# A block kernel with a full-length key buffer, other engines for some steps, and another table of issue

## The chip, the cores and the metric

The kernel runs on one core of one Trainium2 chip. The metric is the device time of one execution in microseconds (us). Three executions of the kernel before took 210.84, 212.09 and 212.49 us; the median is 212.09 us.

The engines are TensorE (PE, and PEld for its weight loads), VectorE (DVE), ScalarE (ACT), GpSimd (POOL) and SyncE (SP), which issues nearly all DMAs. Each runs its own instructions in order and waits on semaphores for the others.

## The reference, cut to what matters

```python
# x: 2048 tokens x 512; H = 32 heads of 16; W, dil = 8, 2; F = 1792
mod = silu(c) @ w_mod                          # six rows: sa, ca, ga, sb, cb, gb
h = layernorm(x) * (1 + ca) + sa
q, k, v = split(h @ wqkv)
# token s attends to the 8 tokens s, s-2, ..., s-14 of its own head
logits = einsum(q, k[s - 2*w]) * 16**-0.5      # masked before token 0
o = einsum(softmax(logits), v[s - 2*w])
x = x + ga * (o @ wo)
h = layernorm(x) * (1 + cb) + sb
h = layernorm(h)
u = gelu(einsum('bsd,sf->bdf', h, w1) + b1)    # mixes the tokens, not the channels
y = einsum('bdf,fs->bds', u, w2) + b2
x = x + gb * transpose(y)
```

Everything is bf16 in memory; sums are kept in f32.

## The kernel before, in words

The 2048 tokens are 16 tiles of 128, in five chunks of 2, 4, 4, 4 and 2 tiles (numbered 0 to 4; SIZES, L255). For each chunk `build_chunk` (L587 to L865) adds the steps below. The name of a step is what the table of issue uses, and a suffix says the engine.

- First norm: `ln1s` (statistics of a tile, DVE or ACT), `rstd1`, `nb1` (minus mean times scale, DVE), `n1_<tile>` (the norm itself; `ln_norm`, L397, on ACT, DVE or POOL). Then transposes, on PE for chunks 0 and 1, by DMA (`xt`) for the others.
- Projections: `qkv<chunk>_<t><j>` with t = 0, 1, 2 for query, key, value; each is four matmuls of 128x128 weights per group of channels. `ev` takes the result from PSUM to the query tile, the key tile `k_f` or the value tile.
- Attention: `qk` (DVE, products of query and shifted keys, a 128x4096 product tile in the four `big` buffers), `red` (PE, sums over the channels of a head), `max` (DVE), `sub` (PE), `exp` (ACT), `esum` (sum of the eight weights, PE, or DVE for chunk 4), `rcp` (ACT), `smB` (DVE), `a2` (four DMAs that spread the weights), `vd` (DMAs that spread the values), `pv` (DVE products), `pvacc` (PE sums), `oev` (copy out of PSUM).
- Output: `wo<tile>` (PE, four matmuls, and a fifth with the identity that adds the residual where `x1` runs on ACT), `x1_<tile>` (back to `xx`).
- Second and third norm: `ln2q`, `ln2m`, `rstd2`, `nb2`, `n2_<tile>`, `aff` (DVE, two passes: times 1 + cb, plus sb), `ln3s`, `rstd3`, `nb3`, `h3_<tile>`.

The token MLP runs over 14 feature tiles: `mlp1_<sweep>_<feature>_<first token tile>` as its tokens become ready, in three sweeps over the tokens, with `park` and `padd` holding partial sums in `gT`; then `gelu`, `mlp2_<token tile>`, `fin` (DVE) and `st_out` (DMA).

Keys of a chunk need the last 16 columns of the chunk before. `k_f` (L308, L309) is a buffer of ten tiles that chunks 3 and 4 write from its start again, so chunk 3 needs a copy of the last 16 key columns of chunk 2, `halo_k3` (L706, ACT). `qk3` reads that copy. For the values there are two buffers and four copies, `halo_v1` to `halo_v4`.

What sets the order of the work is `ORDER` (L180 to L237): one list of all 783 steps, written out in full. `_Graph.schedule` (L87) goes through it, gives out PSUM buffers (six) and product buffers, and the instructions are emitted in exactly this order, so each engine's queue is the list cut down to its engine. A suffix picks the engine: `:a` ACT, `:d` DVE, `:p` POOL, `:s` left out. `:q` has the step's matmuls made as four matmuls of 32 output partitions each (`mm`, L501) in place of one of 128. `warm0` to `warm5` (L507) are matmuls on the identity that compute nothing.

```python
def mm(out, lhsT, rhs, **kw):
    if not G.quad:
        return nc.tensor.matmul(out, lhsT=lhsT, rhs=rhs, **kw)
    for j in range(0, P, 32):
        nc.tensor.matmul(out[j:j + 32], lhsT=lhsT[:, j:j + 32], rhs=rhs, tile_position=(0, j), **kw)
```

Of the kernel before, what the change touches and what calls it, by code (L numbers as in the profile page):

```python
# [185 lines left out]
wsc1_0:p ln1s11:d ln1s6:a ln1v6 ln1s10:d qkv0_00 ev0_00:a qkv0_02 qkv1_03 ln1v9 qkv0_10 rstd1_2 ld_wmod2 ev0_02:a
ln1v11 ev0_10:a nb1_2 n1_7:p ev1_03:a warm3:s qkv1_01 n1_6:a qkv0_12 ld_wmod5 ev0_12:a ln1s13:d ln1s15:a ld_b1
ev1_01:a ln1s14:d qkv1_13 qkv1_11 ev1_11:a qk0_1 qvb1 qk0_0 qkv0_20 red0_0 red0_1 qk0_2 ln1v15 ld_wo0 qkv0_22:q xt6
ev1_13:a ld_wo2 qvb_cp1 ev0_20:a n1_9:p red0_2 ln1v14 ld_wo3 qkv1_23:q qk0_3 red0_3 n1_8:a mask qk1_1 max0 qkv1_00
qkv1_10 ln1v10 xt7 warm5:s ln1s12:a ln1v12 rstd1_4 ln1v13 ev0_22:a vd0_1 ev1_00:a xt8 sub0 exp0 ev1_10:a qk1_3 qk1_0  # L190
qkv1_02 ev1_02:a esum0 rcp0 xt9 smB0 ev1_23:a modrow nb1_4 mrows:a ld_row0 qkv1_12 ev1_12:a qk1_2 wsc1_3:a wsc1_2:a
rstd1_3 nb1_3 n1_10:a wsc2_0:a woq_s qkv1_22 wsc1_1:p red1_0 qkv2_02:q red1_1 red1_2 red1_3 max1 wsc2_2:a qkv1_21:q
a2_0_1 ev1_21:a qkv1_20:q halo_v1:p a2_0_2 sub1 qkv2_12 ev1_20:a exp1 ev2_12:a ev2_02:a qkv2_11 esum1 a2_0_0 a2_0_3
pv0_1 vd0_3 pv0_3 vd0_0 vd0_2 pv0_0 qkv2_03 xt10 n1_12:a xt12 rcp1 pvacc0_0 ev2_11:a pv0_2 qkv2_01 smB1 ev1_22:a
ev2_01:a ld_w1_0_0 pvacc0_1 pvacc0_2 oev0_0:a pvacc0_3 oev0_2:a a2_1_3 wsc2_3:a qk2_2 qkv2_00 ev2_00:a qkv2_10
# [5 lines left out]
vd2_3 oev1_1:a qkv3_20 qkv3_12 ev3_13:a qkv3_02 ln3s1:a oev1_2:a ln3s0:a xt14 wo5 ev3_12:a halo_v3:a qk3_0 xt15
ev3_02:a x1_5:a vd2_0 wo2 x1_2:a ln3v1 wo4 x1_4:a red3_0 ln2q5 smB2 qk3_1 ln2q4 wo3 x1_3:a ln2q3 ln3v0 rstd3_0 qk3_2
vd2_1 ln2q2 a2_2_0 a2_2_3 qkv4_00 qkv3_21 qkv4_12 qk3_3 ev4_12:a qkv4_22 a2_2_1 red3_1 nb3_0 ev4_00:a a2_2_2 h3_0:a
ev3_20:a ev3_21:a vd2_2 ev4_22:a pv2_0 ln2m2 rstd2_2 pv2_1 qkv3_23 qkv4_02 nb2_2 ev4_02:a h3_1:p ev3_23:a qkv3_22
ev3_22:a vd3_2 ln2m4 red3_2 red3_3 max3 pv2_2 pv2_3 n2_3:a n2_2:p pvacc2_0 oev2_0:a sub3 aff2 qk4_3 qkv4_20 exp3
rstd2_4 pvacc2_1 oev2_1:a qkv4_10 ev4_20:a ev4_10:a pvacc2_2 oev2_2:a nb2_4 esum3 rcp3 pvacc2_3 biascols ld_row3
biascols_cp:a n2_5:p vd3_0 vd3_3 oev2_3:a ln3s2:a n2_4:a ln3s3:d ln3v3 wo8 ln3v2 rstd3_2 smB3 a2_3_3 wo9 x1_9:a a2_3_0
nb3_2 h3_2:a wo6 h3_3:a qk4_0 wo7 x1_7:a mlp1_0_1_0 mlp1_0_2_0 halo_v4:a aff4 ln3s5:a qk4_2 ln3s4:d mlp1_0_6_0 vd3_1
red4_0 mlp1_0_5_0:q x1_8:a mlp1_0_3_0:q x1_6:a ln3v5 ln3v4 rstd3_4 ln2q9 qk4_1 red4_1 nb3_4 h3_4:a h3_5:a red4_2
red4_3 mlp1_0_0_0 mlp1_0_0_4 a2_3_2 a2_3_1 vd4_0 mlp1_0_3_4 pv3_1 ln2q8 ld_w2_4 ld_w2_1 ln2q7 mlp1_0_1_4 park0_0:a  # L210
park0_1:a mlp1_0_2_4 ln2q6 park0_2:a max4 mlp1_0_6_4 pvacc3_1 mlp1_0_8_0:q oev3_1:a pv3_3 mlp1_0_5_4:q ld_w1_0_1152
sub4:q ld_w2_3 ln2m6 rstd2_6 exp4 pv3_0 nb2_6 pv3_2 mlp1_0_4_0:q mlp1_0_4_4:q park0_3:a n2_7:p park0_4:a pvacc3_3
oev3_3:a vd4_1 mlp1_0_7_0:q ld_w2_2 pvacc3_0 park0_5:a oev3_0:d n2_6:a mlp1_0_9_0:q n2_8:a pvacc3_2 ld_w1_0_1408
oev3_2:a esum4 park0_6:a wo10 wo11 n2_9:p aff6 rcp4 smB4 a2_4_3 x1_10:a ln2q10 ln3s8:d wo12 ln3s7:d ln3v7 x1_11:a
ln3s6:a ln3s9:d wo13 vd4_3 ln3v8 ln3v6 ln3v9 x1_12:a ln2q12 ln2m10 rstd3_6 ln2q11 a2_4_0 mlp1_0_11_0 nb3_6 h3_8:a
a2_4_1 h3_7:p h3_6:d rstd2_10 x1_13:a mlp1_0_12_0:q warm4:s mlp1_0_10_0:q h3_9:a a2_4_2 mlp1_0_7_4:q vd4_2 ln2m11
rstd2_11 ln2q13 mlp1_0_9_4:q mlp1_0_8_4:q mlp1_0_8_8:q mlp1_0_7_8:q ld_w1_0_1664 park0_7:a park0_8:a ln2m12
mlp1_0_10_4:q pv4_1 mlp1_0_10_8:q pv4_2 nb2_11 mlp1_0_9_8:q mlp1_0_12_4:q mlp1_0_12_8:q n2_11:p ln2m13 pvacc4_2 pv4_3
pvacc4_3 pv4_0 nb2_10 pvacc4_0 pvacc4_1 park0_9:a mlp1_0_11_4:q ld_w1_1_0 rstd2_13 n2_10:d nb2_13 aff10 n2_13:p
rstd2_12 nb2_12 ld_w2_0 mlp1_0_11_8 oev4_2:a ln3s10:d ln3v10 oev4_0:a wo15 park0_10:a aff11 rstd3_10 nb3_10 wo14  # L220
# [10 lines left out]
gelu12 padd1_13 gelu13 mlp2_2_0 mlp2_0_0 mlp2_0_0b ld_w2_7 mlp2_8_0 ld_w2_9 ld_w2_11 mlp2_11_0 ld_w2_15 mlp2_0_0c
fin2_0 mlp2_5_0 fin0_0 mlp2_4_0 st_out0_0 fin4_0 st_out4_0 st_out2_0 mlp2_9_0 fin8_0 mlp2_1_0 fin1_0 st_out1_0
mlp2_3_0 fin3_0 mlp2_7_0 st_out3_0 mlp2_6_0 fin5_0 ld_w2_13 st_out5_0 fin6_0 st_out8_0 st_out6_0 fin9_0 fin7_0
st_out9_0 mlp2_12_0 mlp2_13_0 mlp2_10_0 mlp2_14_0 st_out7_0 fin12_0 st_out12_0 fin11_0 fin13_0 st_out13_0 mlp2_15_0
fin10_0 st_out10_0 fin14_0 st_out11_0 fin15_0 st_out15_0 mlp2_15_2 st_out14_0 fin15_2 st_out15_2 mlp2_15_1 fin15_1
# [775 lines left out]
```

## Time and profile before

| | |
|---|---|
| three executions | 210.84, 212.09, 212.49 us |
| span of the profiled execution, first to last instruction | 207.6 us |
| PE busy | 190.1 us (92%), 1630 matmuls |
| DVE busy | 160.5 us (77%) |
| ACT busy | 128.4 us (62%) |
| POOL busy | 30.6 us (15%) |
| mean granted TensorE clock | 0.999 |
| moved by DMA | 35.93 MB, mean 173 GB/s |

The span leaves out what lies before the first and after the last instruction; the median of the executions is 4.5 us above it. Every instruction is recorded by one helper, so all carry the line L131 and are told apart by their tiles. In lists by time the first two columns are the start and the length in us; "[2.72 <-ACT k_f]" at the end says how long the engine stood idle before and which write released it.

### The profile page before, as it was taken

The page shows a single profiled execution, that of the slowest core. Times are in us where ns is not written, and L with a number is a line of the kernel's source. Part 1 is how long each engine was busy: PE and PEld are TensorE (multiplying, and loading weights), DVE is VectorE, ACT ScalarE, POOL GpSimd, SP SyncE. Part 2 cuts the span into 40 slices and gives each one's busy share as a digit, 9 for nine tenths or more (in the row PEclk, how much of TensorE's full clock was granted, in tenths as well). Part 3 has the DMA queues.
Part 4 walks back from the last instruction along what each step waited for, and adds up shares of the span by engine and source line. Part 5 has one row for each costly group of instructions (what it writes and reads, how often), then busy time and mean ns, then how long its engine had stood idle before and what let it go on. Part 6 is the DMA issues. An engine that isn't in the chain of part 4 may idle for free.

```text
span 207.6 us, 4200 instructions
## 1 busy us (share of the span) xinstructions
PE 190.1 (92%) x1630; PEld 98.4 (47%) x1630; DVE 160.5 (77%) x247; ACT 128.4 (62%) x308; POOL 30.6 (15%) x51
## 2 busy tenths in 40 slices
PE   5898998993999997999989599999999999999992
PEld 5776644441444474444433255444444444444461
DVE  4888999994999999998999869998563024456963
ACT  5769997999579999999889849781662000000000
POOL 4455082000010042010060201220000000000000
PEclk9999999999999999999999999999999999999999
DMA  5999963589979320917996239596995001037221
GB/s 158 321 353 325 240 160 74 186 241 263 303 260 228 106 107 0 335 34 220 256 252 164 84 67 269 112 269 193 305 306 143 0 25 48 7 86 216 76 76 54
DMA packets 55368, 35.93 MB, mean 173 GB/s; under 512 B 24628, under 2 KB 52788, under 8 KB 55348
## 3 DMA queue, kind: packets, MB, share of 16 engines
q1 hardware_dynamic: 55340, 35.66, 61.4%
q8 instruction: 13, 0.21, 0.4%
q14 instruction: 7, 0.06, 0.1%
q10 hardware_dynamic: 8, 0.00, 0.0%
HBM read 22.03 MB, written 2.10 MB: 116 GB/s over the span
## 4 chain that ended last, share of the span: by engine, by line
PE 55%; DVE 14%; ACT 11%; DMA 8%; SPq 6%; issue 4%; DVEq 0%; ACTq 0%
PE psS L131 53%; DVE big L131 11%; SPq L131 6%; DMA wst<-in_A_wqkv_dram 5%; DMA a2sb<-lsb 3%; ACT junk L131 2%; ACT h L131 2%; PE psL L131 2%; ACT xx L131 2%; DVE h L131 1%; ACT gT L131 1%; ACT o_sb L131 1%; DVE m L131 1%; ACT v_sb L131 1%; ACT lsb L131 1%
## 5 line engine op out<-in xcount | busy, mean ns | idle before, releaser
L131 PEld LDWEIGHTS <-wst 128*128 128x128 bf16 (+1 forms) x584 | 35.9, 100 | 36.6 <-issue 5.0
L131 PE MATMUL psS<-h,wst 128*32 128x512 bf16 (+1 forms) x434 | 50.7, 379 | 2.4 <-ACT xx L131 2.3
L131 DVE TENSOR_TENSOR big<-q_sb,k_f 128x4096 bf16<-128x4096 bf16 (+1 forms) x20 | 36.8, 1862 | 2.7 <-ACT k_f L131 2.7
L131 DVE TENSOR_TENSOR big<-a2sb,vD 128x4096 bf16<-128x4096 bf16 (+1 forms) x20 | 37.0, 1880 | 1.5 <-DMA a2sb<-lsb 1.4
L131 DVE SCALAR_TENSOR_TENSOR h<-psS,bcol,rows_bc 128x512 f32<-128x512 f32 (+2 forms) x18 | 12.4, 690 | 22.6 <-PE psS L131 22.3
L131 PE MATMUL psS<-hT,w_qkv 128*128 128x512 bf16 (+2 forms) x192 | 28.9, 354 | 1.0 <-ACT rs L131 1.0
L131 PEld LDWEIGHTS <-w_qkv 128*128 128x128 bf16 (+1 forms) x234 | 19.5, 110 | 17.5 <-issue 4.4
L131 PE MATMUL psS<-gT,big 128*128 128x512 bf16 x112 | 25.0, 379 | 0.0
L131 POOL TENSOR_SCALAR h<-xx,rs,nb 128x512 bf16<-128x512 bf16 x15 | 13.7, 914 | 63.2 <-DVE nb L131 57.6
L131 PEld LDWEIGHTS <-big 128*128 128x128 bf16 x144 | 11.9, 97 | 14.5 <-DMA big<-in_w_mod_dram 1.3
L131 ACT ACTIVATE junk<-xx 128x512 bf16<-128x512 bf16 x26 | 16.3, 628 | 1.6 <-DMA xx<-in_A_x_dram 1.2
L131 PE MATMUL psS<-woq,o_sb 128*128 128x512 bf16 x64 | 16.8, 380 | 0.1
L131 ACT ACTIVATE gT<-psS,bcol 128x512 bf16<-128x512 f32 x14 | 8.7, 685 | 8.5 <-DVE psS L131 8.5
L131 DVE TENSOR_TENSOR psS<-psS,gT 128x512 f32<-128x512 f32 x14 | 9.3, 696 | 5.3 <-PE psS L131 5.3
L131 PEld LDWEIGHTS <-group 128*32 128x32 bf16 x288 | 6.6, 95 | 13.2 <-issue 8.0
L131 ACT ACTIVATE h<-xx,nb,rs 128x512 bf16<-128x512 bf16 x15 | 12.1, 817 | 1.3 <-DVE nb L131 1.3
L131 DVE TENSOR_TENSOR h<-h,xx 128x512 bf16<-128x512 f32 (+2 forms) x18 | 11.4, 633 | 1.8 <-DMA out_dram<-h 1.1
L131 DVE TENSOR_TENSOR h<-h,rows_bc 128x512 bf16<-128x512 bf16 (+2 forms) x20 | 12.1, 605 | 0.3
L131 PE MATMUL psL<-big,group 128*32 128x512 bf16 x128 | 9.1, 381 | 3.3 <-DVE big L131 3.3
L131 PE MATMUL psS<-hT,wst 128*128 128x256 bf16 (+1 forms) x64 | 11.3, 327 | 0.6 <-DMA wst<-in_A_wqkv_dram 0.6
L131 ACT ACTIVATE q_sb<-psS,qvb 128x512 bf16<-128x512 f32 (+1 forms) x20 | 11.4, 597 | 0.2 <-PE psS L131 0.2
L131 ACT ACTIVATE v_sb<-psS,qvb 128x512 bf16<-128x512 f32 (+1 forms) x20 | 11.1, 602 | 0.4 <-PE psS L131 0.2
(93 smaller groups left out, 244.8 us busy)
## 6 DMA issues: line engine op xcount, KB each, us to landing
vD<-v_sb SPq DMA_DIRECT2D x12, 524.5 KB, 4.3
big<-in_B_w_dram SPq DMA_DIRECT2D x4, 896.0 KB, 10.0
vD<-v_sb SPq DMA_DIRECT2D x8, 268.5 KB, 2.5
wst<-in_B_w_dram SPq DMA_DIRECT2D x3, 640.0 KB, 7.2
out_dram<-h SPq DMA_DIRECT2D x15, 128.0 KB, 1.8
xx<-in_A_x_dram SPq DMA_DIRECT2D x7, 256.0 KB, 5.4
wst<-in_B_w_dram SPq DMA_DIRECT2D x2, 800.0 KB, 4.7
gT<-in_w_mod_dram SPq DMA_DIRECT2D x3, 512.0 KB, 9.4
```

The source lines that it names most:

```text
L131: r = fn(*a, **k)
```

## The change

- `k_f` holds the keys of all 2048 tokens: no place is written twice, and `halo_k3` is gone. A projection step that writes two key rows at once is ordered behind the reading of the chunk before.
- The raw value weights lie in a buffer of the second norm (`h2_r[1]`) that is not yet in use, not in a tile of their own.
- A norm on DVE takes (x - mean) * scale, so it doesn't need `nb`; where all norms of a group are on DVE, `nb` can be left out (`:s`, in the table for `nb3_14` and `nb3_15` alone). On POOL and ACT it stays scale and shift.
- `esum` may run on PE or DVE for every chunk and writes PSUM in both cases. In the new table all five are on PE.
- `st_out` may be issued by SP or ACT; eight of eighteen are issued by ACT.
- W2's four pairs of tiles for the `big` buffers may be loaded in any order once all products are summed.
- The warm-up matmuls are 16 to 32 a step: three steps of 16 at the start (before: 48 and 24) and 16 in chunk 3.
- The table is another one throughout. Of the 31 `:q` steps one is left. On other engines than before are, among others: `x1` of tiles 6, 10, 11, 12 and 15 (ACT to DVE, so five identity matmuls go), `halo_v1` and `halo_v2` (POOL to ACT), `n2_3`, `n2_4`, `h3_0`, `h3_2`, `h3_9`, `h3_13` (ACT to POOL), `n2_10` and `h3_10` (DVE to POOL), `ln1s10`, `ln1s13`, `ln3s3`, `ln3s10`, `ln3s12`, `ln3s13` (DVE to ACT), `ln1s1`, `ln1s6`, `ln3s2`, `ln2s14` (ACT to DVE).

```diff
-    k_f = T([P, 4, PAD + P * max(KOFF[c_] + SIZES[c_] for c_ in range(NCH))], BF, "k_f")
+    k_f = T([P, 4, PAD + S], BF, "k_f")
...
-    WARM=(48, 24, 16, 16, 8, 8),
+    WARM=(32, 16, 16, 16, 16, 16),
...
+        if vreads is None:
+            alts.append(("skip", 0.0, lambda: None))
+        nb_op[l, g0] = G.add_any(alts, reads=[("rs", l, g0)] + reads, writes=[("nb", l, g0)], name="nb" + name)
...
+            if by_mean:
+                nc.vector.tensor_scalar(dst, src, m_, r_, op0=ALU.subtract, op1=ALU.mult)
+            else:
+                nc.vector.tensor_scalar(dst, src, r_, n_, op0=ALU.mult, op1=ALU.add)
...
-            wst[0][:, 0:KT * D].rearrange("p (k n) -> p k n", k=KT), T([P, KT, D], BF, "wv_raw"))
+            wst[0][:, 0:KT * D].rearrange("p (k n) -> p k n", k=KT), h2_r[1])
...
-            if t == 1 and ch > 2:
-                ekeys += [("k", c_, j) for c_ in (0, 1) for j in range(j0, j0 + GQ)]
+            if t == 1 and ch > 0 and GQ > 1:
+                ekeys += [("k", ch - 1, j) for j in range(j0 + 1, j0 + GQ)]
...
-        if ch == 2:
-            halo(3, "k")
...
+        G.add_any([("pe", 8 * max(0.06, _t_mm(SB)), f), ("dve", 0.15 + 0.00104 * NW * SB, fd)],
+                  reads=[("lsb", b), "ident"], alloc=s_s, name=f"esum{ch}")
...
+                G.add_any([("sp", 0.5, lambda dst=dst, src=src: nc.sync.dma_start(dst, src)),
+                           ("act", 0.5, lambda dst=dst, src=src: nc.scalar.dma_start(dst, src))],
```

A piece of the table, around the products of chunk 2, before and after:

```diff
-ev2_10:a n1_13:a wo0 wsc2_1:a qk2_1 a2_1_0 n1_14:a a2_1_1 wo1 x1_1:a qkv2_20 ev2_20:a qkv2_13 ev2_13:a halo_k3:a vd1_0
-a2_1_2 qk2_0 red2_0 pv1_0 ev2_03:a qk2_3 x1_0:a qkv2_21 ln2q0 ln2q1 ln2m0 n1_11:p n1_15:a qkv2_23 xt13 pvacc1_0
+ev2_03 rcp1 qkv2_23 n1_12 vd1_1 ev2_13 vd0_3 xt11 vd1_2 qkv2_22 qkv2_12 ev2_22 ev2_02 qk2_1 qk2_0 pvacc0_1 oev0_0 smB1
+pv0_3 qk2_3 ln1v14 red2_0 ev2_12 pvacc0_3 qk2_2 a2_1_1 a2_1_3 halo_v2:a qkv2_20 n1_13:p red2_1 qkv2_21 rstd1_4 ld_row3
```

More of the change, by code (lines that the diff above doesn't have):

```diff
@@ L186 @@
[L186 to L195, printed above, removed]
@@ L201 @@
[L201 to L210, printed above, removed]
@@ L211 @@
[L211 to L220, printed above, removed]
@@ L231 @@
[L231 to L235, printed above, removed]
@@ L236 @@
-st_out15_1
+ident ld_c warm4 ld_x_1_2 cps warm5 ld_x0 ld_x1 act_table ln1s2 silu_exp ln1v2 ln1s1 ln1s0:a ln1v0 ln1v1 rstd1_0 ln1s3
+nb1_0 ln1v3 warm3 silu_dve consts ld_x_1_4 ln1s4 ln1s5:a ln1v5 ld_x_2_6 ld_wmod1 ld_wmod0 ld_x_2_8 ln1v4 ln1s7 warm2:s
+n1_0 rstd1_1 nb1_1 modcols1 n1_4:d a1col n1_1:p ln1s6 ld_wqkv0 tr0_0 hT0_1:d n1_3 modcols0 n1_5 sab n1_2:p tr1_2 ln1s8
+hT0_0 hT0_2 tr1_0 wsc0_0:p hT1_2 ld_wqkv1 hT0_3:d ln1s9 hT1_0 hT1_1:d qkv0_00 ln1v9 wsc0_3:p hT1_3 ld_x_3_10 ln1v6
+ln1v7 ld_x_4_14 wsc0_1 ln1v8 ld_wqkv2 ld_wmod3 qvb0 qvb_cp0 rstd1_2 nb1_2 qkv1_03 qkv0_10 ev0_00:d ev1_03 wsc0_2
@@ new lines @@
+qkv1_21 red1_0 red1_1 smB0 a2_0_2 wsc1_1:p qk1_2 red1_2 red1_3 wsc2_3:a woq_s wsc1_3:a qkv2_01 ev1_20 a2_0_0 wsc1_0:a
+a2_0_3 nb1_3 ev1_22 qkv2_11 ev1_23 max1 a2_0_1 sub1 halo_v1:a ev1_21 ev2_01 n1_10 ev2_11 qkv2_10 wsc2_0:a exp1 qkv2_00
+qkv2_02 ev2_10 vd0_2 pv0_1 esum1 wsc2_2:a pv0_2 vd0_0 pv0_0 ev2_00 qkv2_03 pvacc0_0 n1_11 xt10 pvacc0_2 vd1_3 qkv2_13
+ev2_03 rcp1 qkv2_23 n1_12 vd1_1 ev2_13 vd0_3 xt11 vd1_2 qkv2_22 qkv2_12 ev2_22 ev2_02 qk2_1 qk2_0 pvacc0_1 oev0_0 smB1
+pv0_3 qk2_3 ln1v14 red2_0 ev2_12 pvacc0_3 qk2_2 a2_1_1 a2_1_3 halo_v2:a qkv2_20 n1_13:p red2_1 qkv2_21 rstd1_4 ld_row3
@@ new lines @@
+a2_1_0 a2_1_2 oev0_2 ev2_23 nb1_4 wo1 x1_1 ln2q1 wo0 x1_0 ev2_21 ev2_20 pv1_3 red2_2 red2_3 xt13 xt12 n1_15 max2 ln2q0
+ld_b1 vd1_0 pv1_1 n1_14 qkv3_03 xt14 qkv3_13 qkv3_02 ev3_02 ln2m0 qkv3_10 ev3_10 qkv3_20 ld_row2 pvacc1_1 rstd2_0
+ev3_20 oev1_1 ev3_03 qkv3_12 qkv3_00 ev3_13 ev3_00 ld_row1 xt15 pvacc1_3 oev1_3 pv1_0 pv1_2 sub2 exp2 pvacc1_0 ev3_12
+pvacc1_2 oev1_2 nb2_0 biascols biascols_cp qk3_0 qk3_2 esum2 n2_0 vd2_3 rcp2 qkv3_11 qkv3_01 oev1_0 qkv3_23 wo2 n2_1
+smB2 wo3 halo_v3:a wo4 ev3_01 qkv3_21 qk3_3 ev3_11 qkv3_22 x1_2 ln2q2 x1_3 vd2_1 aff0 ln2q3 qkv4_00 ln2m2 qk3_1 ev3_23
@@ new lines @@
+ld_w1_0_896 red3_0 qkv4_02 x1_4 red3_1 a2_2_1 wo5 red3_2 red3_3 a2_2_0 qkv4_12 ln2q4 rstd2_2 ev3_22 ln3s0:a vd2_0
+a2_2_2 nb2_2 ln3s1:a x1_5 a2_2_3 pv2_0 ln2q5 ev3_21 pvacc2_0 vd2_2 pv2_3 ld_w1_0_512 ln2m4 ev4_12 qkv4_22 max3 n2_2:p
+ln3v0 qkv4_20 ln3v1 rstd2_4 n2_3:p aff2 oev2_0 nb2_4 ev4_22 sub3 ev4_02 pv2_2 exp3 n2_5 pv2_1 esum3 rstd3_0 rcp3 smB3
+n2_4:p qkv4_10 ln3s3:a ln3v3 ev4_10 pvacc2_3 pvacc2_2 ln3s2 oev2_2 ln3v2 oev2_3 nb3_0 ld_w2_1 h3_0:p warm1 aff4
+ld_w1_0_0 pvacc2_1 oev2_1 wo8 ev4_00 rstd3_2 wo9 qk4_1 wo6 nb3_2 ln3s4 x1_6:d h3_1 ln3s5:a wo7 h3_3 h3_2:p mlp1_0_2_0
@@ new lines @@
+ln3v4 ld_w2_3 ln3v5 a2_3_3 x1_8 a2_3_2 rstd3_4 vd3_3 qk4_0 nb3_4 mlp1_0_3_0 a2_3_0 x1_7 h3_4 h3_5 mlp1_0_1_0 a2_3_1
+x1_9 ln2q7 ev4_20 ln2q8 ln2q9 mlp1_0_0_0 qk4_2 vd3_2 mlp1_0_3_4 red4_0 red4_1 red4_2 mlp1_0_0_4 vd3_1 ln2q6 park0_0
+pv3_3 mlp1_0_1_4 mlp1_0_2_4 pv3_2 ld_w2_0 ln2m6 mlp1_0_6_0 mlp1_0_6_4 mlp1_0_5_0 park0_1 rstd2_6 qk4_3 nb2_6 park0_2
+n2_7 park0_3 vd3_0 pv3_1 mlp1_0_4_0 pvacc3_3 n2_6 pvacc3_2 red4_3 mlp1_0_4_4 oev3_2 ld_w1_0_1152 mlp1_0_5_4 mlp1_0_8_0
+ld_w1_0_1408 n2_8 max4 pv3_0 park0_4 sub4 mlp1_0_10_0 oev3_3 halo_v4:a exp4 park0_5 pvacc3_1 n2_9:p pvacc3_0 esum4
@@ new lines @@
+oev3_1 mlp1_0_7_0 aff6 oev3_0 park0_6 vd4_2 wo13 ln3s7 ln3s8 ln3v8 rcp4 ln3s9 vd4_0 ln3v7 ln3s6:a wo10 vd4_3 wo12
+x1_13 ln2q13 ln3v6 wo11 x1_10:d ln3v9 rstd3_6 nb3_6 x1_12:d smB4 ln2q10 h3_6 ln2m13 rstd2_13 ln2m10 h3_8:d h3_7:p
+x1_11:d ln2q12 rstd2_10 ln2q11 mlp1_0_9_0 ln2m12 mlp1_0_11_0 nb2_10 a2_4_0 a2_4_3 nb2_13 mlp1_0_8_4 mlp1_0_7_4
+rstd2_12 h3_9:p a2_4_1 mlp1_0_7_8 park0_7 mlp1_0_10_4 mlp1_0_8_8 ln2m11 n2_10:p nb2_12 aff10 mlp1_0_11_4 mlp1_0_10_8
+mlp1_0_9_4 mlp1_0_9_8 a2_4_2 n2_13:d rstd2_11 nb2_11 pv4_3 ln3s10:a park0_8 park0_9 mlp1_0_12_0 mlp1_0_12_4 vd4_1
@@ new lines @@
+mlp1_2_4_11 gelu7 mlp1_2_5_11 mlp1_2_5_14 padd2_0 gelu0 padd2_5 mlp1_2_4_14 padd2_4 mlp1_1_11_10 mlp1_1_12_10 gelu6
+gelu4 gelu5 padd1_11 gelu11 padd1_12 gelu12 big_done mlp2_0_0 mlp2_0_0b ld_w2_11 gelu13 mlp2_1_0 ld_w2_5 mlp2_5_0
+fin1_0 st_out1_0:a mlp2_0_0c ld_w2_13 mlp2_4_0 mlp2_11_0 ld_w2_9 fin5_0 fin0_0 st_out0_0 fin4_0 mlp2_2_0 fin2_0
+st_out2_0 mlp2_9_0 st_out5_0:a fin9_0 ld_w2_7 mlp2_3_0 mlp2_6_0 fin6_0 st_out9_0:a fin3_0 st_out6_0:a mlp2_10_0
+fin10_0 mlp2_13_0 st_out3_0 mlp2_7_0 fin7_0 st_out4_0 ld_w2_15 mlp2_8_0 st_out7_0 fin8_0 st_out8_0:a mlp2_14_0 fin11_0
@@ L307 @@
     q_r = ring(NB, [P, 4 * CM], BF, "q_sb")
-    KOFF = [T0[c_] if c_ < 3 else T0[c_] - T0[3] for c_ in range(NCH)]
-    k_f = T([P, 4, PAD + P * max(KOFF[c_] + SIZES[c_] for c_ in range(NCH))], BF, "k_f")
+    k_f = T([P, 4, PAD + S], BF, "k_f")
     v_r = ring(2, [P, 4 * (CM + PAD)], BF, "v_sb")
@@ L417 @@
     wraw = (wst[2][:, 0:KT * D].rearrange("p (k n) -> p k n", k=KT),
[L418 to L419 removed]
+            wst[0][:, 0:KT * D].rearrange("p (k n) -> p k n", k=KT), h2_r[1])
+    wkey = ([("wst", 2)], [("wst", 0)], [("h2", 1, i) for i in range(KT)])
     def ld_w(t):
@@ L492, in halo @@
                    ("dve", 0.15, lambda: nc.vector.tensor_copy(v_, u_))],
-                  reads=[(nm, ch - 1, j) for j in range(4)],
-                  writes=[("kh", 3)] + [("k", -1, j) for j in range(4)] if nm == "k" else [("vh", ch), ("vh", ch - 2)],
-                  name=f"halo_{nm}{ch}")
+                  reads=[("v", ch - 1, j) for j in range(4)], writes=[("vh", ch), ("vh", ch - 2)], locks=True,
+                  name=f"halo_v{ch}")
     add("pool", 2.0, mk_consts, writes=["consts", "mask"], name="consts")
@@ L718, in f @@
                                         op=ALU.mult)
-            add("dve", _t_tt2(NW * C), f, reads=[("q", bq, dlo), ("k", ch, dlo)] + ([("kh", 3)] if ch == 3 else [("k", ch - 1, dlo)]), alloc=s_,
+            add("dve", _t_tt2(NW * C), f, reads=[("q", bq, dlo), ("k", ch, dlo), ("k", ch - 1, dlo)], alloc=s_,
                 locks=True, name=f"qk{ch}_{dlo}")
@@ L930 @@
                     copy2(gT[:, ft, :], lambda s_=s_: ps(s_), D, False, [], [("gT", ft), "gT_use"], f"park{li}_{ft}", frees=s_)
+    G.add("skip", 0.0, lambda: None, writes=["big_use"], name="big_done")
     homes = ([(w_r[t][:].rearrange("p k n -> p (k n)"), 1, [("w_qkv", t, kt) for kt in range(KT)]) for t in (1, 0, 2)] +
              [(hT_r[i][:], 1, [("hT_raw", i)] + [("hT", i, kt) for kt in range(KT)]) for i in range(NHT)] +
-             [(big_r[i][:], 2, ["big_use"]) for i in range(NBIG)])
+             [(big_r[i][:], 2, []) for i in range(NBIG)])
     s_lo = 0
@@ L944 @@
         wkey = ("w2", s_lo)
-        dma(w2p, w2_view[:, :, s_lo * P:(s_lo + ns) * P], P * NFT * ns * P * 2, [], wkeys + [wkey], f"ld_w2_{s_lo}",
+        dma(w2p, w2_view[:, :, s_lo * P:(s_lo + ns) * P], P * NFT * ns * P * 2, ["big_use"] if not wkeys else [], wkeys + [wkey], f"ld_w2_{s_lo}",
             rate=(0, 220e3, 290e3)[ns], row=ns * 256)
```

91 lines of the change are left out of this document (45 added, 46 removed).

## The prediction, made before the change was run

> **What bounds the kernel now.** I read the page's 40 slices first, then busy times by stretch.
>
> ```profile
> PE   5898998993999997999989599999999999999992
> DVE  4888999994999999998999869998563024456963
> ACT  5769997999579999999889849781662000000000
> ```
>
> ```profile
> 60.00:70.00 10.00, 10.00 (x100) 4.71 (x100) 9.97 (x9) 9.88 (x23) 0.00 (x0) 1.00 0.69 195
> 110.00:117.00 7.00, 4.74 (x33) 1.80 (x32) 6.00 (x18) 6.84 (x24) 0.93 (x1) 1.00 0.49 140
> 130.00:150.00 20.00, 20.00 (x95) 9.00 (x94) 16.82 (x42) 11.76 (x31) 3.07 (x4) 1.00 0.75 217
> ```
>
> The columns are stretch, length, then busy us (instructions) of PE, weight loads, DVE, ACT and POOL, the clock, the DMA share and GB/s. Up to about 117 us three engines are full together; after that PE alone. The chain of waits ends accordingly:
>
> ```profile
> 116.41 0.59 ACT xx L131 x2
> 117.00 0.04 issue
> 117.04 86.50 PE psS L131 x569
> ```
>
> From 117.04 us PE runs to 203.54 without a wait, so the end is fixed by when PE has its inputs at about 117 us and by how much PE work is left. The list of who waited for whom names PE's two long stops and one of DVE:
>
> ```profile
> PE psL L131 <- DVE big L131: 3.3, 1, 3.3
> DVE big L131 <- ACT k_f L131: 2.7, 1, 2.7
> PE psS L131 <- ACT xx L131: 2.3, 1, 2.3
> ```
>
> The first two are one event, seen in the instructions in order of time:
>
> ```profile
> 44.55 2.28 DVE L131 TENSOR_TENSOR big<-q_sb,k_f 128x4096 bf16<-128x4096 bf16 x1
> ...
> 49.27 0.26 ACT L131 ACTIVATE k_f<-k_f 128x64 bf16<-128x64 bf16 x1
> ...
> 49.55 2.29 DVE L131 TENSOR_TENSOR big<-q_sb,k_f 128x4096 bf16<-128x4096 bf16 x1 [2.72 <-ACT k_f L131]
> ...
> 51.90 0.40 PE L131 MATMUL psL<-big,group 128*32 128x512 bf16 x4 [3.30 <-DVE big L131]
> ```
>
> The copy k_f<-k_f is halo_k3. It belongs to chunk 3, yet qk2_0 waits for it: its own operands were out at 45.5 us by the order of ACT's queue. DVE stands 2.72 us, PE 3.30.
>
> **The change part by part.** I counted each engine's instructions in both tables, with the mean time of its row, up to fixed steps.
>
> *Full-length keys.* The copy goes, and with it DVE's 2.72 us. What is late next is ev2_00, the operand of qk2_0: in the new table ACT has 40.6 us of instructions up to and with it, before 43.3 up to ev2_10, which came last then, so it isn't later. Taken: -2.7 on DVE; bounds 0 (another wait fills it) and -2.7.
>
> *DVE's order.* The last product of chunk 4 (pv4_0) ended at 122.0 us with 118.2 us of DVE instructions up to it; the new table has 122.0 up to it. The 3.8 more are x1 of tiles 6, 10, 11, 12 (4 x 0.69), aff10 (0.92) and norms and their small scalars now ahead of it, less esum4 (1.02), oev3_0 (0.68) and statistics moved to ACT. Successive DVE instructions overlap (instruction times add to 171.6 us, busy is 160.5), so 3.8 is 3.6 on the clock. In the old trace that DVE had no gap of note from 52 to 97 us, so all of it counts: +3.6.
>
> *The start.* SP issues 9 loads before the key weights, not 11; 256 KB less lie ahead of them, about 0.8 us at the 339 GB/s of the stretch from 10 to 20 us. This hides: DVE has the same statistics to do. DVE begins with a tile of x, not with silu, which filled the wait for x (2.90 to 3.62): +0.4 on DVE.
>
> *New waits of DVE in the new table.* woq_s needs the first modulation row. Its step mrows, which started at 29.7 us, has 28.0 us of ACT work ahead of it, before 27.6; the row's DMA takes 3.7 us (the group of rows_bc), so it lands near 35, about when DVE, which came there at 34.1, has its 0.5 us more done: 0 to 1.0, taken 0.5. ln2m2 follows qk3_3 and aff0 directly while two x1 and two ln2q (4 x about 0.8 on ACT) still run: 0 to 1.0, taken 0.5. So +1.0.
>
> pv4_0 then ends at 122.0 - 2.7 + 3.6 + 0.4 + 1.0 = 124.3 us. Before, PE took it up at 124.38, since its stop at 114.7 to 117.0 (a PSUM buffer held until x1_13) had put it behind DVE. In the new table ACT has 116.8 us of work up to x1_13, not 122.7, and PE will wait for DVE instead. pvacc4 ended about 125.25 before; now 124.3 + 0.45 = 124.75: -0.5.
>
> *PE work after pvacc4* falls from 77.9 to 76.8 us by the same count (identity matmul of wo15 0.22, and feature steps that now stand ahead): -1.1. Over the kernel PE's sum falls 1.5: five identity matmuls (5 x 0.216), 8 warm-up matmuls (8 x 0.081), less esum4 on PE (+0.25).
>
> *Whole matmuls.* Price of a four-fold step, and of a change between the two kinds:
>
> ```profile
> 60.39 0.60 PE L131 MATMUL psL<-m,nident 128*32 128x512 bf16 x8
> 60.82 1.90 PE L131 MATMUL psS<-hT,w_qkv 128*32 128x512 bf16 x32
> 62.65 0.62 PE L131 MATMUL psS<-lsb,ident 128*128 128x128 bf16 x8
> ```
>
> 32 quarter matmuls start 1.83 us before what follows; eight whole ones need 8 x 0.216 = 1.73 and the change to the other kind is the remaining 0.10. Between 60.39 and 60.82 there is no change, and 0.43 is exactly two rounds. So a step costs the same either way and a change about 0.1. The tables have 38 and 40 changes: +0.2.
>
> *Edits at nothing.* Norm by the mean: one DVE instruction either way (0.40 to 0.41 before); the form isn't in the trace, +/-0.1 each bounds six of them at +/-0.6. The raw value weights' new home is first needed by n2_2, near 76 us, and is read last near 40. esum4 on PE: eight short matmuls (0.25) with mlp1 behind it. Stores by ACT: ACT does nothing after about 150 us; its one DMA took 0.56 us to issue, SP's 0.4 to 0.6. Cost 0, gain up to 0.5 at the last stores. ld_w2_7 is queued on SP behind st_out2, which waits for fin2; its use, mlp2_7, comes five token tiles (5 x 3.02 us) later against the 10.0 us from issue to landing of these loads. ld_w2_13 waits on SP for the last sweep, with ld_w2_9 and the first stores behind it; ld_w2_9 has five token tiles too. The moved halo_v copies cost ACT 0.25 each and leave POOL.
>
> Sum on PE's end: -0.5 - 1.1 + 0.2 = -1.4: 203.5 becomes 202.1, the span 206.2, and with the 4.5 between this span and the median of the runs **210.7 us**.
>
> **Rivals.**
>
> *GpSimd norms wait for DVE's products (slower).*
>
> ```profile
> 75.70 2.81 POOL L131 TENSOR_SCALAR h<-h,rs,nb 128x512 bf16<-128x512 bf16 x1 [15.93 <-DVE nb L131]
> 80.89 0.77 POOL L131 TENSOR_SCALAR h<-xx,rs,nb 128x512 bf16<-128x512 bf16 x1 [2.38 <-DVE mv L131]
> 105.28 3.43 POOL L131 TENSOR_SCALAR h<-xx,rs,nb 128x512 bf16<-128x512 bf16 x2 [15.27 <-DVE nb L131]
> ```
>
> A norm that takes 0.77 us beside a DVE reduction takes 2.81 beside a product, ending 0.7 after the product's end. The new table puts n2_2 and n2_3 (before aff2), n2_4 (aff4), n2_9 (aff6) and n2_10 (aff10) on POOL, and DVE waits for each. If each pass begins only when the products end, DVE loses 2 x 0.77 + 3 x 0.77 = 3.85 us: 210.7 + 3.9 = 214.6. Against it: max3, ln3s2 and max4, which leave POOL free, stand before three of the four. It decides once these waits exceed 1.4 us, and means over 1% slower from 3.5.
> [...]
>
> *The gap's worth is nil.* If another engine holds DVE for as long (ACT is 9.9 of 10 us busy from 60 to 70), the keys bring nothing and only x1's moves act: about 212.1.
>
> *The remaining waits go too.* DVE stood 4.7 us besides the keys' gap before pv4. If the new order spares half of it, PE ends 2.1 us earlier: 208.6.
>
> *A cold PE.* The old start has 72 warm-up matmuls in 5.86 us, the first at about 0.107 apart, the last at 0.056. The new one has 48, and PE then idles about 2.7 us before modcols1. If it falls back to half pace, qkv0_00 and qkv1_03 take 0.86 longer each: 212.4. Against it: the idle 3.30 us at 48.6 left the clock at 1.00.
> [...]
>
> **How the numbers follow.** The forecast (small gain, by itself 208.6 to 212.5) has 0.45, GpSimd's waits 0.27, nil 0.13, the better order 0.10, the cold PE 0.05. About 1% (2.1 us) is what a measurement of this kernel tells from no change. Faster by more (under 210.0): 0.4 of the forecast, all of the better order and a little else, 0.31. Slower by more (over 214.2): nine tenths of GpSimd's waits, tails of the others, 0.29. Within: 0.40. The range of 8 in 10 goes from 208.0, under the better order, to 215.6, GpSimd's waits with 1 us for the bounds of the new waits.
>
> **What would show it.** The 2.72 us before qk2_0 gone; pv4_0 ending near 124.3 and PE's last stop in front of pvacc4 or close to it; PE's end near 202.1; POOL norms before aff2 and aff6 under or over 2 us and DVE's idle time there; matmul spacing at 13 us. I am wrong if DVE's idle time up to pv4_0 exceeds 8 us, or if PE waits for weights after 130 us.

## The result and the profile after

Four executions of the changed kernel took 205.37 to 206.42 us, median 206.03, beside 212.29 of the kernel before (210.84 to 214.38): a ratio of 0.971 [0.966, 0.976]. On another chip it was 205.38 beside 212.46, 0.967 [0.963, 0.970]. The brackets after a ratio are its 95% interval; the ratios here and below leave out executions that are more than 1.5% above the fastest of their kernel, the medians are of all. The predicted 210.7 is 4.7 us too long, and the time lies under the range of 208.0 to 215.6.

The profiled execution has a span of 204.3 us; its own time was 206.04, 1.7 us above the span. First its 40 slices, with the row of the granted clock:

```profile
PE   7599999998999999689999999999999999999994
DVE  1788999899999999999999899997380462261695
ACT  4695999896799999989999888863472000000000
PEclk9958999999999999999999999999999999999999
```

The hole that TensorE (PE) had in the tenth slice is gone. At the start something is new: the granted clock is 0.5 and 0.8 of full speed in the third and fourth slice, from 10 to 20 us. The stretches that the prediction showed:

```profile
60.00:70.00 10.00, 9.77 (x69) 4.32 (x68) 10.00 (x7) 9.88 (x23) 0.00 (x0) 1.00 0.73 213
110.00:117.00 7.00, 6.99 (x33) 3.12 (x32) 6.37 (x25) 6.22 (x22) 2.29 (x3) 1.00 0.09 17
130.00:150.00 20.00, 20.00 (x94) 9.11 (x93) 15.38 (x34) 10.68 (x24) 2.57 (x4) 1.00 0.88 242
```

From 110 to 117 us PE is busy 6.99 of 7 us, before 4.74: its stop for the PSUM buffer that `x1_13` frees is gone too. The chain of waits ends so, and the list of waits of PE begins so:

```profile
118.80 2.36 DVE big L131 x2
121.30 2.28 DVE big L131 x2
123.62 77.65 PE psS L131 x400
```

```profile
PE psS L131 <- DVE big L131: 2.4, 5, 1.0
PE psS L131 <- DMA big<-in_w_mod_dram: 2.0, 1, 2.0
PE psS L131 <- ACT lsb L131: 1.7, 1, 1.7
```

PE's last stop is in front of pvacc4 and VectorE (DVE) ends it, as predicted. From there it runs to 201.26 us (202.1 predicted, 203.54 before). Behind PE's end 3.0 us are left, before 4.1. In all, the span is 3.3 us shorter and the time 6.3. So about half of the gain is not in a comparison of these two profiles at all.

### The profile page after: what moved, and what is told of

The parts are those of the page before. It is cut to its first block, busy times and chain, and to the rows that moved or that the text cites. A ratio compares the mean times of both kernels' runs of the same rounds, so it can differ in the third digit from the quotient of the medians.

```text
span 204.3 us, 3562 instructions
## 1 busy us (share of the span) xinstructions
PE 192.4 (94%) x1310; PEld 97.8 (48%) x1310; DVE 161.6 (79%) x251; ACT 129.3 (63%) x310; POOL 32.8 (16%) x48
## 4 chain that ended last, share of the span: by engine, by line
PE 47%; DVE 25%; ACT 11%; DMA 7%; issue 4%; SPq 3%; DVEq 0%; ACTq 0%
PE psS L131 46%; DVE big L131 17%; DVE h L131 4%; ACT junk L131 3%; SPq L131 3%; DMA gT<-in_w_mod_dram 3%; ACT h L131 3%; DMA a2sb<-lsb 2%; DMA xx<-in_A_x_dram 2%; DVE m L131 1%; DVE mv L131 1%; DVE st L131 1%; DVE lsb L131 1%; ACT q_sb L131 1%; PE psL L131 1%
## 5 line engine op out<-in xcount | busy, mean ns | idle before, releaser
L131 PE MATMUL psS<-h,wst 128*128 128x512 bf16 x224 | 50.2, 379 | 0.1
L131 POOL TENSOR_SCALAR h<-xx,rs,nb 128x512 bf16<-128x512 bf16 x13 | 20.6, 1590 | 76.2 <-PE psS L131 36.7
L131 PE MATMUL psS<-hT,w_qkv 128*128 128x512 bf16 (+1 forms) x144 | 28.5, 346 | 0.0
L131 PEld LDWEIGHTS <-w_qkv 128*128 128x128 bf16 x186 | 19.4, 111 | 16.8 <-issue 3.4
L131 PEld LDWEIGHTS <-big 128*128 128x128 bf16 x144 | 12.0, 99 | 15.4 <-DMA big<-in_w_mod_dram 2.1
L131 ACT ACTIVATE h<-xx,nb,rs 128x512 bf16<-128x512 bf16 x17 | 13.6, 810 | 0.2 <-DVE nb L131 0.2
L131 PE MATMUL psS<-hT,wst 128*128 128x256 bf16 (+2 forms) x76 | 12.7, 359 | 0.0
L131 DVE BATCH_NORM_STATS2 st<-xx 128x6 f32<-128x512 bf16 x12 | 8.2, 685 | 5.1 <-DMA xx<-in_A_x_dram 5.1
L131 ACT ACTIVATE q_sb<-psS,qvb 128x512 bf16<-128x512 f32 (+1 forms) x18 | 10.7, 618 | 2.5 <-DVE w_qkv L131 2.0
L131 PEld LDWEIGHTS <-ident 128*128 128x128 bf16 (+1 forms) x115 | 9.0, 118 | 6.4 <-issue 3.2
L131 ACT ACTIVATE junk<-h 128x512 bf16<-128x512 bf16 x18 | 11.3, 627 | 1.2 <-DVE h L131 0.8
```

Source lines behind the costliest of these rows:

```text
L131: r = fn(*a, **k)
```

## The experiments

"Full keys" below means the parts of the change's diff that concern `k_f`, the order of its writers and the raw value weights, with the step `halo_k3` gone. Ratios are to the kernel before, run on the same chip.

**The kernel before once more, the keys alone, whole matmuls alone.** These have the table of before; the second has the full keys, the third no `:q`.

```diff
-    k_f = T([P, 4, PAD + P * max(KOFF[c_] + SIZES[c_] for c_ in range(NCH))], BF, "k_f")
+    k_f = T([P, 4, PAD + S], BF, "k_f")
...
-        if ch == 2:
-            halo(3, "k")
```

> The kernel before, unchanged, timed and profiled again. Its profiled execution had a span of 207.6 us, 4.7 us under the median of its runs (212.3); the changed kernel's runs lie 1.7 us over their spans. Theory: the profiled execution was a quick one, and the runs of this kernel have spans near 210.5, 1.7 under their times. Rival: its spans are near 207.6 throughout and 4.7 us lie outside the span in this kernel, 1.7 in the changed one.

> The kernel before with the keys kept for all tokens (and the raw value weights in the second norm's buffer, without which it doesn't fit), nothing else. The copy of the last key columns and its wait are gone. Theory: DVE's 2.7 us idle before the third product of chunk 2 goes and half or more reaches the end, 1.3 to 2.7 us faster. Rival: ACT holds the residual adds as before, PE's stop near 117 us only grows, and the time stays within 0.5 us.

> The kernel before with all 31 four-fold steps made as whole matmuls, the table else the same. Theory from the trace: a step costs the same either way, a change between the kinds 0.1 us, so within 0.5 us of before. Rival: the 370 more PE instructions and weight loads of the four-fold steps make its executions slower than the profiled one, and 2 to 3 us go.

Before again: 212.97 (210.95 to 214.03), ratio 1.001 [0.997, 1.005], and its profile has a span of 210.0, not 207.6, with 1.7 us around it. Why is the first profile of before 2.4 us shorter? PE after its stop of 3.30 us, in the first profile of before:

```profile
52.45 1.92 PE L131 MATMUL psS<-hT,w_qkv 128*128 128x512 bf16 x8
54.30 0.61 PE L131 MATMUL psS<-big,group 128*32 128x512 bf16 x8
```

and in the second, with the line of the stretch from 52 to 58 us below it:

```profile
51.83 1.04 PE L131 MATMUL psL<-big,group 128*32 128x512 bf16 x8 [3.30 <-DVE big L131]
52.81 3.60 PE L131 MATMUL psS<-hT,w_qkv 128*128 128x512 bf16 x8
56.34 1.04 PE L131 MATMUL psS<-big,group 128*32 128x512 bf16 x8
```

```profile
52.00:58.00 6.00, 5.94 (x25) 1.46 (x19) 4.97 (x5) 1.38 (x5) 0.00 (x0) 0.51 0.96 298
```

The same eight matmuls take 3.60 us, not 1.92, at a granted clock of 0.51. The stop is the same; what follows it isn't. The mean granted clock of the other executions of before tells how usual that is (71 that the ratios count, over five batches): 0.976 in 8, median 213.4 us; 0.983 or 0.984 in 42, 212.4; 0.988 to 0.992 in 21, 211.5; none higher. The profile that I predicted from had 0.999, and its span of 207.6 with 1.7 us around it makes about 209.3 us (an estimate), less than any of these executions took (the quickest 209.83).

The keys alone: 209.37 (209.01 to 209.76), ratio 0.988 [0.985, 0.990], 2.5 to 3 us less, at a clock of 0.992 in all four. Whole matmuls alone: 211.5, ratio 0.997 [0.992, 1.002], not told from nothing.

**A filler in PE's stop (before, wait left as it is).** 32 warm-up matmuls stand in front of `red2_0`.

```diff
-a2_1_2 qk2_0 red2_0 pv1_0 ev2_03:a
+a2_1_2 qk2_0 warm5:p red2_0 pv1_0 ev2_03:a
...
-    WARM=(48, 24, 16, 16, 8, 8),
+    WARM=(48, 24, 16, 16, 8, 32),
```

> Before, unchanged but for 32 warm-up matmuls on the identity (8 before, elsewhere) right in front of red2_0, in the 3.30 us in which PE waits for the first product of chunk 2. The wait of VectorE for the copy of the old keys stays, so no engine gets its inputs earlier. Theory (the half clock after the stop is a part of what the full keys saved): the slow matmuls at 52 to 57 us are gone, 1.5 to 2.5 us less than before, ratio 0.988 to 0.993. Rival (the full keys saved VectorE's 2.72 us and nothing else): no change, 0.998 to 1.002, or a little slower where the filler holds red2_0 up.

208.94 (208.11 to 209.71), ratio 0.983 [0.978, 0.987]: 3.5 us less, more than expected, at a clock of 0.997 to 1.000 in all six executions. Their spans, 206.5 to 208.1, are like that of the rare execution of before, 207.6. From its instructions in order of time:

```profile
49.68 1.95 PE L131 MATMUL psS<-ident 128*128 128x128 bf16 x32
53.14 0.62 PE L131 MATMUL psL<-big,group 128*32 128x512 bf16 x8 [1.51 <-DVE big L131]
53.69 1.92 PE L131 MATMUL psS<-hT,w_qkv 128*128 128x512 bf16 x8
```

PE gets its first product no earlier (53.14 here), yet the next eight matmuls take 1.92 us. Matmuls that compute nothing bring as much as the full keys do. So what the full keys brought, in this table, is nearly all the clock.

**The keys with a filler at the next stop.** With the full keys the half clock comes later, after the stop for `x1_13`:

```profile
111.35 2.02 PE L131 MATMUL psS<-h,wst 128*128 128x512 bf16 x20
115.81 9.21 PE L131 MATMUL psS<-h,wst 128*32 128x512 bf16 x136 [2.45 <-ACT xx L131]
```

(9.21 us for the 136 quarter matmuls; 7.52 in the kernel before, at full clock.) 32 warm-up matmuls that write the logits' PSUM buffer go into that stop.

> The keys alone, with 32 warm-up matmuls on the identity, written to the logits' PSUM buffer, in the 2.45 us in which PE waits at 113.3 us for the buffer that x1_13 frees. Theory (after that stop the clock halves and costs 1.7 us): the granted clock is 1.00 (0.992 before the filler) and the time 207.4 to 208.2, 1.2 to 2 us less than the keys alone (209.37). Then the keys at full clock stand 0.7 to 1.5 us under the filled kernel before (208.94), which is what VectorE's 2.72 us are worth by themselves: less than their length, since PE waits for x1_13 anyway. Rivals: the gap is worth its whole length (206.2 to 206.6); or no change by the filler (209.0 to 209.7).

208.97 (208.03 to 209.19), ratio 0.987 [0.980, 0.994], clock 0.989 to 1.000. In its profile:

```profile
114.19 1.96 PE L131 MATMUL psL<-ident 128*128 128x128 bf16 x32
116.71 7.52 PE L131 MATMUL psS<-h,wst 128*32 128x512 bf16 x136 [0.55 <-ACT xx L131]
```

The quarter matmuls are back at 7.52 us. But the filler gains 0.4 us in the medians, which the intervals don't tell from nothing, not 1.2 to 2: the theory's size fell, and the rival of no change came closer. And beside the filled kernel before (208.94, on the same chip) the full keys, and with them DVE's 2.72 us, show no gain.

**x1_13 earlier.** In the table of before with the full keys, `x1_13` moves ahead of five steps on ScalarE (ACT); the second kernel also has eight stores issued by ACT.

```diff
-x1_12:a ln2q12 ln2m10 rstd3_6 ln2q11 a2_4_0 mlp1_0_11_0 nb3_6 h3_8:a a2_4_1 h3_7:p h3_6:d rstd2_10 x1_13:a mlp1_0_12_0:q
+x1_12:a x1_13:a ln2q12 ln2m10 rstd3_6 ln2q11 a2_4_0 mlp1_0_11_0 nb3_6 h3_8:a a2_4_1 h3_7:p h3_6:d rstd2_10 mlp1_0_12_0:q
```

> The keys alone, with x1_13 moved ahead of five steps on ScalarE (ln2q12, rstd3_6, ln2q11, h3_8, rstd2_10; about 3.2 us), nothing else. Theory (TensorE's stop of 2.45 us at 113.3, for the buffer that x1_13 frees, and the half clock behind it are on the path, and are a large part of what after has over the keys alone): the stop falls under 0.6 us, the granted clock is 1.00, pvacc4 comes 1 to 2.5 us earlier, and the time is 207.0 to 208.3, 1 to 2.4 us under the keys alone (209.37). Rival (VectorE sets pvacc4 and the stop only moves to it): 208.8 to 209.6.

> As e12, with eight of the eighteen stores issued by ScalarE, the same eight as in after. Theory (the stores at the end queue on SyncE): the end of TensorE stays and the time behind it falls from about 4 to about 3 us: 0.7 to 1.1 us under e12. Rival (the tail belongs to the order of the last sweep): within 0.3 us of e12.

206.58 (205.94 to 206.95), ratio 0.974 [0.969, 0.978], 2.8 us under the keys alone by one moved word. PE in order of time:

```profile
111.71 3.52 PE L131 MATMUL psS<-h,wst 128*128 128x512 bf16 x48
115.47 6.01 PE L131 MATMUL psS<-h,wst 128*32 128x512 bf16 x108 [0.23 <-POOL h L131]
121.29 1.06 PE L131 MATMUL psS<-big,group 128*32 128x256 bf16 x32
```

The stop of 2.45 us has become 0.23, and the sums of chunk 4's products begin at 121.29 us, with the keys alone at 124.84. With the stores on ACT: 206.75, ratio 0.975 [0.971, 0.979], so they bring nothing there.

**Order alone, without the full keys.** The kernel before, with `halo_k3`, the filler in front of `red2_0`, and `x1_13` earlier.

> Before, with its short keys and halo_k3, and two edits of its table alone: the 32 warm-up matmuls in front of red2_0 (as in e5) and x1_13 ahead of five steps on ScalarE (as in e12). VectorE still waits 2.72 us for halo_k3. Theory (PE's clock after its stop, and the buffer that x1_13 frees, are what counts; the gap on VectorE by itself is not on the path): 206.3 to 207.3, as fast as e12 with its full keys (206.58). Rival (the gap is covered only while x1_13 holds PE up, and counts in full once that is gone): 208.5 to 209.5, no gain by the second edit.

208.11 (207.58 to 208.75), ratio 0.980 [0.976, 0.984]. It lies between theory and rival. PE:

```profile
52.54 0.62 PE L131 MATMUL psL<-big,group 128*32 128x512 bf16 x8 [1.51 <-DVE big L131]
...
123.68 0.62 PE L131 MATMUL psS<-big,group 128*32 128x256 bf16 x16 [0.74 <-DVE big L131]
```

Now DVE is late: PE waits for the last product at 123.68. The four kernels make a table, all at a granted clock of 0.99 to 1.00:

| | `x1_13` as before | `x1_13` earlier |
|---|---|---|
| short keys, filler | 208.94 | 208.11 |
| full keys | 208.97 (filler at the stop for `x1_13`) | 206.58 |

Each edit alone brings 0.0 or 0.8 us; both together 2.4, about the length of either wait (2.72 and 2.45). The four ran on three chips, and the ratios are 0.983, 0.980, 0.987 and 0.974 with intervals that overlap in part, so the sizes are rough. The profiles show the mechanism: PE at pvacc4 needs DVE's last product as well as its own earlier work. With the full keys and a filler the product was out at 121.84 us and PE came to it at 124.04. With `x1_13` earlier and short keys PE was there first, and the product ended at 123.62. With both edits these times are 121.26 and 121.29. The two waits stand side by side: one holds DVE, the other PE and its buffers.

**x1 on ACT or on DVE.** Once the changed kernel with `x1` of tiles 6, 10, 11, 12 and 15 back on ACT, once the keys alone with these five on DVE.

```diff
-x1_13 ln2q13 ln3v6 wo11 x1_10:d ln3v9 rstd3_6 nb3_6 x1_12:d
+x1_13 ln2q13 ln3v6 wo11 x1_10 ln3v9 rstd3_6 nb3_6 x1_12
```

> After, with x1 of tiles 6, 10, 11, 12 and 15 back on ScalarE and their five identity matmuls back on TensorE; the table is otherwise that of after. Theory (a part of the gain of after over the keys alone is that x1_13 comes earlier on ScalarE, so that PE no longer stops for its PSUM buffer at 115 to 120 us): PE stops again for x1_13 by 1 to 2.5 us and has 1.1 us more work: 1 to 3 us slower than after, 207 to 209 us. Rival (VectorE is the bound up to pv4_0, and loses 4 times 0.69 us here): same or up to 2 us faster than after.

> The keys alone, with x1 of tiles 6, 10, 11, 12 and 15 on VectorE as in after and their five identity matmuls gone; the table is otherwise that of before. Theory (ScalarE's sums, not VectorE's work, hold up chunk 4, so 3.5 us more work of VectorE shortens the time): x1_13 comes 2 us earlier, PE's stop at 113.3 shrinks to under 1 us, the clock stays, and the time is 206.5 to 208, 1.5 to 3 us less than the keys alone (209.37). Rival (my prediction's step, VectorE's 3.6 us count in full): 1 us slower to no change.

Back on ACT: 209.15 (207.87 to 209.96), ratio 0.984 [0.978, 0.989], 3.1 us slower than after. The size was expected, the place was not: PE doesn't stop for `x1_13`. DVE, with less work, waits for ACT's sums:

```profile
115.48 0.17 DVE L131 SCALAR_TENSOR_TENSOR nb<-mv,rs 128x4 f32<-128x4 f32 x1 [1.24 <-ACT rs L131]
...
118.97 0.16 DVE L131 TENSOR_TENSOR mv<-mv,sums 128x1 f32<-128x1 f32 x1 [1.20 <-ACT junk L131]
```

On DVE in the table of before: 212.02 (209.12 to 213.19), ratio 1.000 [0.995, 1.005], 2.6 us slower than the keys alone; here the theory fell outright. The ten executions lie far apart: the six that the ratio counts have a median of 210.6, 1.2 us above the keys alone. In its profile the stop for `x1_13` is as long as ever (2.50 us), and PE already waits for the moved `x1` before it:

```profile
110.05 1.02 PE L131 MATMUL psS<-woq,o_sb 128*128 128x512 bf16 x4 [1.23 <-DVE xx L131]
...
112.25 1.02 PE L131 MATMUL psS<-h,wst 128*128 128x512 bf16 x4 [0.96 <-DVE xx L131]
```

But this profile is of the quickest of the ten, at a clock of 1.000, with a span of 207.4 us beside 207.3 for the keys alone. What the other nine lose is not shown by it. So the other engine is neither good nor bad by itself: in the order of after it saves 3 us, in that of before it gains nothing and costs 1 to 2.6.

**Norms back from GpSimd (POOL) to ACT.** The changed kernel with `n2_3`, `n2_4`, `h3_0` and `h3_2` on ACT.

> After, with the norms n2_3, n2_4, h3_0 and h3_2 on ScalarE again, not on GpSimd (2.7 to 5.5 us each there, beside VectorE's products). Theory (VectorE doesn't wait for GpSimd, and ScalarE is the fuller of the two): the same to 1.5 us slower. Rival of the prediction (VectorE waits for GpSimd's slow norms): 1 to 4 us faster.

207.94 (207.77 to 208.99), ratio 0.979 [0.974, 0.985], 1.9 us slower than after: the rival fell. In the profile of after the second norms on POOL are as slow as it said, and slower, while `h3_0` and `h3_2` took 1.07 and 0.77 us; POOL, then DVE:

```profile
74.95 5.53 POOL L131 TENSOR_SCALAR h<-xx,rs,nb 128x512 bf16<-128x512 bf16 x2 [36.69 <-PE psS L131]
82.70 5.32 POOL L131 TENSOR_SCALAR h<-xx,rs,nb 128x512 bf16<-128x512 bf16 x1 [2.21 <-issue]
```

```profile
81.06 1.41 DVE L131 TENSOR_TENSOR h<-h,rows_bc 128x1024 bf16<-128x1024 bf16 x2
...
88.81 1.86 DVE L131 TENSOR_TENSOR h<-h,rows_bc 128x1024 bf16<-128x1024 bf16 x2
```

A norm lies beside two products for 5.32 us, but it ends 0.6 and 0.8 us before the pass (`aff2`, `aff4`) that needs it, and DVE has no gap there: in between stand `max3` and the statistics of the third norm. With the four norms on ACT, DVE waits 1.0 us for a query tile that ACT writes, a wait that it doesn't have in the profile of after.

**Stores issued by SyncE (SP) again, in the changed kernel.**

> After, with all eighteen stores issued by SyncE as before. After's span ends 3.0 us behind PE's last matmul, before's 4.1. Theory (the stores on ScalarE save about 1 us at the very end): the time behind PE's end grows by 0.7 to 1.1 us, and the time with it, to about 207. Rival (that difference lies in the last sweep's order): no change, within 0.3 us.

206.82 (206.07 to 207.20), ratio 0.974 [0.969, 0.978]. Behind PE's end its profile has 4.0 us, after's 3.0; in the times this is 0.8 us, with intervals that overlap after's. The other table showed nothing, so this stays open at 0 to 1 us.

**The start.** The changed kernel has 48 warm-up matmuls at the start, mostly at half pace (3.46 us for the last 32, 1.95 for as many in the filler), and then PE waits 1.97 us:

```profile
8.79 0.55 PE L131 MATMUL psS<-sc,big 128*128 128x1 bf16 x16 [1.97 <-DMA big<-in_w_mod_dram]
...
11.36 2.16 PE L131 MATMUL psS<-ident,h 128*128 128x128 bf16 x16 [0.29 <-POOL h L131]
```

Sixteen transposes take 2.16 us; a kernel with 72 warm-up matmuls in place of the last 16, which fill that wait, has 1.05. It ran twice, and once with `exp3` moved as well.

> The changed kernel with 72 instead of 16 matmuls in the third warm-up step, so that PE is kept busy until the modulation weights land. In the changed kernel the granted clock was 0.66 in the stretch from 10 to 20 us, and its first projections took twice as long. Theory: with the clock kept, the first products of DVE start about 1.5 us earlier and 0.5 to 1.5 us reach the end. Rival: the loads of x and of the key weights set that start, and nothing moves (within 0.4 us).

> After with 72 warm-up matmuls in place of 16 in the last step ahead of the first transposes, as in the run after_warm, and exp3 ahead of the two evictions ev4_22 and ev4_02 on ScalarE, so that TensorE's stop of 1.69 us in front of esum3 at 83 us gets shorter. If that stop is on the path: 0.5 to 1.5 us under the warm kernel (204.69), 203.2 to 204.2. If VectorE, which doesn't wait for esum3 then, sets the end of chunk 4: 204.4 to 205.0. In both cases faster than before by 3.4 to 4.3%.

> The changed kernel, unaltered, on this chip: 205.4 to 206.5, granted clock 0.983, for the comparison with e14 on the same chip.

> The run after_warm again (72 warm-up matmuls in place of 16 in the last step ahead of the first transposes), for an interval against the changed kernel on the same chip. Theory (two stretches at half clock before 20 us cost 1 to 1.5 us): 204.3 to 205.2, 0.8 to 1.6 us under e15. Rival (the start hides it): within 0.4 us of e15.

First 204.69, ratio 0.968 [0.964, 0.973]; with `exp3` moved 205.02, 0.969 [0.964, 0.974]; then, beside the changed kernel on one chip (205.38), 205.54, 0.967 [0.962, 0.972]. In the profile of that last run PE waits at 14 us for the key weights, and behind it the clock is at half again, by the mean of 0.992 over the span for about 3.3 us (an estimate; its row of the clock has 0.7 from 15.4 to 20.5 us). Eight matmuls that take 1.06 us in the first run take 1.54:

```profile
14.20 1.54 PE L131 MATMUL psS<-hT,wst 128*128 128x256 bf16 x8 [1.79 <-DMA wst<-in_A_wqkv_dram]
```

In the first run the stop at this place was 1.69 us, and the clock stayed at 1.00. So a gain by a longer warm-up is not shown, and neither is a version that beats the changed kernel by more than the intervals.

## Why the prediction was wrong

**The term that failed** is the last of the sum: "with the 4.5 between this span and the median of the runs". I took it for a constant. In nine executions of ten here the time is 1.6 to 1.9 us above the span, in the new kernel 1.7. The other 2.8 were no overhead: they were the difference between a rare execution of before (clock 0.999) and the usual one (0.976 to 0.992). The profile of the new kernel has no half clock behind 16.8 us, and the one at its start costs less than the runs can tell. With 1.7 the sum gives 206.2 + 1.7 = 207.9.

**The sentence behind it** is "the idle 3.30 us at 48.6 left the clock at 1.00", which I used against the cold PE. It was true of one execution. The mean clock of all the 71 others, 0.992 or less, is that of at least one stretch at half pace, the second profile shows it at that stop, and the filler shows that this costs some 3.5 us. The same stop of 3.30 us came with half clock in one profile and without it in another. Half clock also followed shorter stops: one of 2.45 us with the keys alone, stops of 1.97 and 0.43 us at the start of after, and one of 1.79 us with the longer warm-up. Behind stops of 2.30 and 2.44 us in the two profiles of before, those for `x1_13`, PE ran at full pace (136 quarter matmuls in 7.52 us). What decides which it is, the runs don't show.

**Full keys, -2.7 on DVE.** The gap is gone, as predicted, and no other wait took its place: added up from the gaps in the trace, DVE stands idle 4.3 us between its first instruction and the last product (7.4 in the first profile of before, about 10 in the second). What it is worth I had wrong twice: by itself nothing that the runs can tell (208.97 against 208.94), with `x1_13` earlier some 1.5 us in the medians (ratios 0.980 and 0.974, with intervals that overlap) and 2.4 at the end of the last product (123.62 and 121.26 in the two profiles), and through PE's clock about 3. The rival that its worth is nil was right for the old order alone; its 212.1 had no working, and the sum without the 2.7 gives 213.4.

**x1_13.** "ACT has 116.8 us of work up to `x1_13`, not 122.7, and PE will wait for DVE instead" is what happened, and I booked only -0.5 for pvacc4. With the full keys, moving `x1_13` alone brought 2.8 us. I had counted DVE's moved work (+3.6) in full and missed that this work is what frees ACT: with it on ACT, DVE waits instead.

**DVE up to pv4_0**, predicted to end at 124.3: 123.58. The moved work was sized right: DVE is busy for 114.0 us up to there, before 110.4, which is the +3.6. It began 0.8 us later (3.73 against 2.90), not 0.4. The waits were wrong: DVE's idle time fell by about 3 us (7.4 to 4.3), where the sum had 1.7 (-2.7 and +1.0). This is the way of the rival "the remaining waits go too", which had 0.10. **PE's end** 202.1, measured 201.26. **Behind it** 4.1 kept, measured 3.0. These last two sizes are the other 1.9 us: 207.9 - 0.8 - 1.1 = 206.0.

**GpSimd's norms**, 0.27: the price on POOL was right or low: a norm took 2.81 us beside one product and 0.77 beside a reduction in before, and 5.32 beside two products in after. The waits of DVE are not there, and with four of the norms back on ACT the kernel is 1.9 us slower. **A cold PE**, 0.05: it came, at the start (a granted clock of 0.66 from 10 to 20 us); its price stays under what the runs can tell. **Whole matmuls**, +0.2: nothing measurable, as booked. **The stores**, 0 to 0.5: 0 in one table, 0 to 1 in the other.

What would have shown me wrong looked at one side only: DVE's idle time and PE's weights stayed good. A time below the range had no such test, because the offset was not questioned; the three times of before (210.84 to 212.49) beside a span of 207.6 were the sign.

**The account**, by medians: 212.3 before; 209.4 with the full keys (nearly all by PE's clock: the filler without them gives 208.9); 206.6 with `x1_13` earlier; 206.0 and 205.4 with the rest (GpSimd, stores, whole matmuls, shorter warm-up, and a half clock at the start), a last step that the intervals don't tell apart.
